# The last convolution pieces handed on inside SBUF, and the last gate moved to the activation, in an S4D and token-mixer kernel

## The chip, the cores and the metric

The kernel runs on one core of a Trainium2 chip. The metric is the device time of one execution in microseconds; smaller is better. The kernel before was run three times: 697.69 us median, 696.94 to 703.69. Inputs and outputs are float32 in HBM.

The engines named below: TensorE (PE in the profile) multiplies matrices, VectorE (DVE), ScalarE (ACT) and GpSimd (POOL) work on elements, SyncE (SP) only issues DMA transfers, which 16 DMA engines carry out. Each engine takes its instructions in the order in which they stand; engines wait for each other through semaphores.

## The reference, cut to what matters

L is 2048 tokens, D is 448 channels, N is 256 states, F is 1792.

```python
x = A_u
mod = (_silu(c) @ w_mod).reshape(c.shape[0], 6, 1, -1)
sa, ca, ga, sb, cb, gb = (mod[:, k] for k in range(6))

# first half: a state-space layer, computed as a long convolution over the tokens
h = _layernorm(x) * (1 + ca) + sa
K = 2.0 * jnp.einsum("dn,dnl->dl", C, jnp.exp((A * dt[:, None])[:, :, None] * pos)).real
y = jnp.fft.irfft(jnp.fft.rfft(h_t, 2 * L) * jnp.fft.rfft(K, 2 * L), 2 * L)[:, :, :L]
x = x + ga * (y + h * D_skip)

# second half: an MLP over the token axis, shared by the channels
h = _layernorm(_layernorm(x) * (1 + cb) + sb)
u = _gelu(jnp.einsum("bsd,sf->bdf", h, w1) + b1)
x = x + gb * (jnp.einsum("bdf,fs->bds", u, w2) + b2)
```

The layer norm is taken twice before the MLP, once outside and once in the mixer. `gb` (in the kernel `mod[5]`) scales channels; the MLP mixes tokens and leaves the channels apart.

## The kernel before, in words

**Up to about 350 us** the kernel makes the convolution kernel K from the state-space parameters (`st_step`, `st_kgen`), transforms it and the normalised input with matrices of sines and cosines, and leaves the transformed input in the HBM tensor `us_d`. The channels are taken in two halves of 224 (`DC`), c = 0 and c = 1.

**The pieces.** Per half there are 16 pieces (`NP`), n = 0 to 31 in all; piece n holds two of the 32 rows k of the outer transform. For a piece, `pc_load` (L768) brings its input `u` and its tables `si`, three pieces ahead, in rings of three and four buffers. `pc_s2` multiplies (`kx`, L804), VectorE makes two products (`z`, L812), `pc_inv` transforms back (`vv`, L820 and L821), and `pc_out` (L823) has ScalarE copy the values from PSUM to the tile `vt` and stores them to the HBM tensor `v_d` (L828). In the second half ScalarE also makes a swapped copy of u (`pc_swap`), and GpSimd builds two of the tables (`pc_tables`, L795 to L797). The pieces of the first half run inside the work on K. Those of the second run in the loop `for k in range(NP + 1)` from L1171.

**The order of SP's queue.** All of these transfers are issued by SP. Up to k = NP - 4 a planner places them; from there on (`tc.manual_schedule(engines={ENG.SP})`) they stand as written. The order of the other engines is written out by hand throughout. At k = NP - 3 SP issues the first weight block of the MLP (`wst.load`, L186) and the first pair of x blocks (`x_pair`, L1166), after the loop the second weight block.

**The token blocks.** The second half of the kernel goes over 16 token blocks, r = 0 to 15, of 128 tokens. `ln_load` (L1228) reads block r's values from `v_d` into a tile `vt` (128 partitions: the 32 rows k times 4; two groups g of 448). `ln_y` (L1246) finishes the inverse transform with the table `ft`, two matmuls, one per group, into one PSUM tile `y`, of which there is a single buffer; VectorE adds it to x and sums the row (L1253). `stats` (L1237) makes the mean on VectorE and then, on ScalarE, the sum of squares of (value - mean) and its root. `ln_mod` applies the gate and takes the second sum and `stats`; `ln_out` writes the normalised block as a rounded part `h3h` and a remainder `h3l`, so that three fast matmuls replace a full-precision one. In front of the first blocks stand matmuls on `acc[6]` that nobody reads (`warm`, L1291: nine, one and two of them before y(0), y(1) and y(2)).

**The MLP.** `WeightStream` loads weight blocks of 128 x 896 (ring of three), and splits each into `whi` (ScalarE, L206) and `wlo` (VectorE, L215). The first sweep runs over the 16 token blocks for the first 896 of the hidden units (`mlp1`, seven PSUM banks, 21 matmuls a block) with the normalisation in between; then `gelu` (L1332) empties the banks into `uh[0]` and `ul[0]` through a ring `u` of three buffers; a second sweep does the other 896 units and `gelu` fills `uh[1]` and `ul[1]`. The third sweep makes 16 output blocks of 128 tokens, each from kh = 0 and kh = 1 (21 matmuls each), and ends each with

```python
V.scalar_tensor_tensor(y, o, b2[:, t : t + 1], mod[5], ALU.add, ALU.mult)
V.tensor_tensor(y, y, xt, ALU.add)
nc.sync.dma_start(out[0, ss], y)
```

where `xt` is the block's x after the first half, parked in HBM (`x2_d`) during the second sweep.

## Time and profile before

| what | value |
|---|---|
| runs of the kernel | 697.69 us median (696.94 to 703.69, three runs) |
| the profiled execution, its own time | 699.5 us |
| its span | 697.7 us |
| TensorE busy | 646.5 us (93%) |
| ScalarE busy | 448.5 us (64%) |
| VectorE busy | 424.1 us (61%) |
| GpSimd busy | 274.7 us (39%) |
| mean granted TensorE clock | 0.988 of full speed |
| HBM traffic | 91.46 MB read, 34.87 MB written, 181 GB/s over the span |

The span runs from the first instruction to the last event of one profiled execution; the time of that execution is somewhat longer than its span. Lines such as L1250 are lines of the kernel before. In the rows of a timeline the columns are: start in us, duration in us, engine, line, operation, output <- inputs, shapes, how many instructions were merged, and in brackets how long the engine had been idle and what ended the wait. "SPq" is SP issuing a transfer; the transfer itself ends later. Adjacent matmuls overlap in the records, so starts tell the pace better than durations. A name such as `w` stands for all buffers of that tile.

### The profile page before, as it was taken

Reading aid. Unit: us, or ns where it says so; the run is one execution under the profiler, and the core shown is the slowest. Engines: PE = TensorE matmul, PEld = TensorE weight load, DVE = VectorE, ACT = ScalarE, POOL = GpSimd, SP = SyncE. Lnnn points to the kernel's source line nnn. Section 1 sums busy time; section 2 is a strip of 40 time slices with the busy share of each in tenths; the row PEclk is TensorE's granted clock in tenths of the full one; section 3 lists DMA queues with packets and bytes.
Section 4 is the critical chain, followed back from the end, with each engine's and each line's share of the span. In section 5 each row is a group of like instructions: output and inputs, shape, how many; then the busy total and the mean of one; then the engine's idle time right before and its main releaser. Section 6 shows DMA issues by size and latency. Waiting matters only on the chain.

```text
span 697.7 us, 18532 instructions
## 1 busy us (share of the span) xinstructions
PE 646.5 (93%) x7314; PEld 486.1 (70%) x7314; DVE 424.1 (61%) x811; ACT 448.5 (64%) x841; POOL 274.7 (39%) x364
## 2 busy tenths in 40 slices
PE   0868999999988899999999989999999999999997
PEld 0444454455545676676789747778999999999996
DVE  7877889787575584857744368777622354444431
ACT  5787698899879899999766568877422332222220
POOL 6694669588588767777546200000000000000000
PEclk9998999999999999999999999999999999999999
DMA  7595647588785486554579899974683445555640
GB/s 183 178 194 143 214 163 241 212 234 268 213 266 165 126 170 170 145 157 120 142 235 301 257 278 244 236 177 135 174 247 108 146 132 159 159 158 165 169 129 28
DMA packets 101894, 128.04 MB, mean 184 GB/s; under 512 B 13547, under 2 KB 85231, under 8 KB 101807
## 3 DMA queue, kind: packets, MB, share of 16 engines
q1 hardware_dynamic: 100606, 123.31, 63.0%
q0 software_dynamic: 1200, 3.54, 2.4%
q8 instruction: 58, 0.95, 0.6%
q14 instruction: 30, 0.24, 0.1%
HBM read 91.46 MB, written 34.87 MB: 181 GB/s over the span
## 4 chain that ended last, share of the span: by engine, by line
PE 68%; ACT 10%; DMA 8%; DVE 6%; issue 4%; POOL 3%; SPq 1%; DVEq 0%; ACTq 0%; POOLq 0%
PE xe L621 7%; PE acc L1222 7%; PE o L1365 6%; PE o L1364 6%; PE o L1366 6%; PE acc L1223 6%; PE acc L1224 6%; PE kg L711 6%; DMA si<-in_SK_dram 3%; PE xg L621 3%; PE pu L542 2%; PE pu L574 2%; PE vv L820 2%; PE kx L804 2%; PE vv L821 2%
## 5 line engine op out<-in xcount | busy, mean ns | idle before, releaser
L206 ACT CAST whi<-w 128x896 fp32r<-128x896 f32 x64 | 59.8, 938 | 134.9 <-PE o L1365 84.6
L215 DVE TENSOR_TENSOR wlo<-w,whi 128x896 fp32r<-128x896 f32 x64 | 68.1, 1088 | 43.1 <-ACT whi L206 36.8
L684 POOL TENSOR_TENSOR G<-mag,gs 128x512 f32<-128x512 f32 x56 | 71.9, 1283 | 50.9 <-ACT gs L680 47.1
L1222 PE MATMUL acc<-h3h,whi 128*128 128x448 f32 x224 | 82.7, 369 | 0.8 <-ACT h3h L1273 0.8
L1223 PE MATMUL acc<-h3l,whi 128*128 128x448 f32 x224 | 81.5, 364 | 0.7 <-DVE h3l L1280 0.5
L1365 PE MATMUL o<-ul,whi 128*128 128x448 f32 x224 | 81.3, 363 | 0.0
L1364 PE MATMUL o<-uh,whi 128*128 128x448 f32 x224 | 81.2, 362 | 0.0
L1224 PE MATMUL acc<-h3h,wlo 128*128 128x448 f32 x224 | 80.7, 360 | 0.0
L1366 PE MATMUL o<-uh,wlo 128*128 128x448 f32 x224 | 80.6, 360 | 0.0
L711 PEld LDWEIGHTS kg<-E,G 128*32 128x32 f32 x3584 | 56.6, 114 | 32.3 <-issue 22.2
L711 PE MATMUL kg<-E,G 128*32 128x64 f32 x3584 | 66.4, 228 | 6.7 <-issue 6.1
L685 POOL TENSOR_TENSOR G<-mag,gs 128x512 f32<-128x512 f32 x56 | 71.8, 1282 | 0.0
L621 PE MATMUL xg<-tab,lph 64*128 64x512 f32 x112 | 62.3, 556 | 5.1 <-ACT gs L680 2.4
L621 PE MATMUL xe<-tab,lph 64*128 64x512 f32 x112 | 62.2, 555 | 1.1 <-ACT gs L681 0.9
L686 DVE TENSOR_TENSOR E<-m,xe 128x512 f32<-128x512 f32 x53 | 36.4, 687 | 41.3 <-ACT xe L679 24.3
L1368 DVE SCALAR_TENSOR_TENSOR y<-o,b,mod 128x448 f32<-128x448 f32 x16 | 10.9, 684 | 80.2 <-PE o L1366 80.2
L665 POOL TENSOR_TENSOR m<-mag,w 128x512 f32<-128x512 f32 x53 | 56.0, 1056 | 4.3 <-DMA u<-us_d 0.2
L1222 PEld LDWEIGHTS acc<-h3h,whi 128*128 128x128 f32 x224 | 42.0, 188 | 13.9 <-ACT h L1278 5.6
L812 DVE TENSOR_TENSOR z<-kx,u 128x448 f32<-128x448 f32 x48 | 28.4, 620 | 27.7 <-PE kx L804 27.7
L1223 PEld LDWEIGHTS acc<-h3l,whi 128*128 128x128 f32 x224 | 42.1, 188 | 3.3 <-DVE h3l L1280 0.8
L1364 PEld LDWEIGHTS o<-uh,whi 128*128 128x128 f32 x224 | 42.0, 188 | 3.4
L621 PE MATMUL xe<-tab,lex 64*128 64x512 f32 x56 | 28.9, 531 | 16.6 <-DMA lex<-wm 15.8
(233 smaller groups left out, 1512.1 us busy)
## 6 DMA issues: line engine op xcount, KB each, us to landing
w<-in_B_w_dram SPq DMA_DIRECT2D x64, 224.0 KB
w<-in_B_w_dram SPq DMA_DIRECT2D x32, 448.0 KB
u<-us_d SPq DMA_DIRECT2D x48, 224.0 KB
yu_d<-yt SPq DMA_DIRECT2D x16, 448.0 KB
yi<-yu_d SPq DMA_DIRECT2D x32, 224.0 KB
us_d<-uo SPq DMA_DIRECT2D x16, 448.0 KB
v_d<-vt SPq DMA_DIRECT2D x32, 224.0 KB
vt<-v_d SPq DMA_DIRECT2D x16, 448.0 KB
```

What stands on the lines that cost most here:

```text
L206: self.nc.scalar.copy(hi, w)
L215: eng.tensor_tensor(lo, w, hi.bitcast(F32), ALU.subtract)
L621: T.matmul(out[k], lhs[r], rhs[r], start=start, stop=stop)
L684: G.tensor_tensor(Gt[:, 1], mg_, v32(sg), ALU.mult)
L685: G.tensor_tensor(Gt[:, 0], mg_, v32(cg_), ALU.mult)
L711: T.matmul(kg[32 * q : 32 * q + 32, m], Gt[:, c, d], E[:, c, d], start=h == 0 and c == 0 and m == 0, stop=h == 1 and c == 1, skip_group_ch ...
L1222: nc.tensor.matmul(acc[f], hi[:, fs], h3h[:, r], start=r == 0, stop=False)
L1223: nc.tensor.matmul(acc[f], hi[:, fs], h3l[:, r], start=False, stop=False)
L1224: nc.tensor.matmul(acc[f], lo[:, fs], h3h[:, r], start=False, stop=r == 15)
L1364: nc.tensor.matmul(o, hi[:, ks], uh[kh][:, k], start=kh == 0 and k == 0, stop=False)
L1365: nc.tensor.matmul(o, hi[:, ks], ul[kh][:, k], start=False, stop=False)
L1366: nc.tensor.matmul(o, lo[:, ks], uh[kh][:, k], start=False, stop=kh == 1 and k == 6)
```

## The change: the first two blocks, the squares and the last gate

1. **The first two token blocks.** The tables of the inverse transform are reordered so that within a piece's 128 rows the block number r is outermost. So block r's rows of a piece lie together, `v_d` is read in runs of two groups (3584 bytes a partition), and the rows of blocks 0 and 1 are the first 16 partitions of each `vt` of `pc_out`. For the last four pieces (n = 28 to 31; k = 24 to 31 of the second half of the channels) SP copies these 16 partitions to an SBUF tile `vlast` before it stores the piece to `v_d`. Blocks 0 and 1 read from `v_d` what was stored earlier: the last rows of the first half in four short transfers, and all of k below 24 in one (`v_load(r, end)`). `ln_y` makes their `y` from four matmuls of 224 columns with `ft` and two with a new table `fl` (128 KB) on `vlast`.
2. **Places in SP's order.** The first two weight blocks and the first pair of x blocks are written ahead of the loop, in the part that the planner places; the second pair of x blocks stands before blocks 2 and 3. In the order that results, the two weight blocks and the first pair are issued behind the u load that stood at 353.10 us, ahead of the tables of piece 19; the four short transfers ahead of the u load of piece 21.
3. **`warm`.** One, two and two matmuls instead of nine, one and two.
4. **`stats`.** ScalarE squares (total - D * value) straight from the row sum, with the scale taken out at the root; the mean is made on VectorE behind that.
5. **The last gate.** `gelu` multiplies the activation by `mod[5]` on VectorE before it is split; in the second half ScalarE makes the rounded part, one slice behind. The third sweep's end multiplies the bias and adds x (in place) without waiting for the matmuls, and then adds the product.

```diff
-    order = lambda a: a.reshape(P, 32, 2, 2, 2, 16).swapaxes(3, 4)
+    order = lambda a: a.reshape(P, 32, 2, 2, 2, 16).transpose(0, 1, 5, 2, 4, 3)
...
+    fl = np.zeros((4, 2, 4, 2, 2, 2, 2, 64))
+    for r in range(2):
+        for g in range(2):
+            fl[:, r, :, g, r, :, g] = t["FT"][-32:].reshape(4, 2, 4, 64).swapaxes(1, 2)
+    t["FL"] = fl.reshape(64, 2 * 2 * P)
...
             rows = v_d[2 * p : 2 * p + 2, :, c * DC : (c + 1) * DC]
+            late = n - 2 * NP + 4
+            if late >= 0:
+                nc.sync.dma_start(vlast[16 * late : 16 * late + 16], vt[0:16])
             nc.sync.dma_start(rows.rearrange("k p d -> p k d"), vt)
...
+        v_v = v_d.rearrange("k (r ch g) d -> r k ch g d", ch=4, g=2)
+        end = 2 * NP - 8
+        wst.load()
+        wst.load()
+        x_pair(0)
+        vlast = swp.tile([64, 2, DC], F32, name="vlast", bufs=1)
+        fl = swp.tile([64, 2, 2, P], F32, name="fl", bufs=1)
+        vts = {}
+
+        def v_tile(r):
+            vts[r] = rot.tile([P, 2, D], F32, tag="vt", name="vt", bufs=4)
+
+        def v_load(r, k):
+            nc.sync.dma_start(vts[r][0 : 4 * k].rearrange("p g d -> p (g d)"), v_v[r, 0:k].rearrange("k ch g d -> k ch (g d)"))
+
         pc_swap(NP)
         for k in range(NP + 1):
...
-            if k == NP - 3:
-                wst.load()
-                x_pair(0)
-
-        wst.load()
+            if k == 1:
+                nc.sync.dma_start(fl.rearrange("p r j m -> p (r j m)"), i["FL"])
+                for r in range(2):
+                    v_tile(r)
+                    for g in range(2):
+                        nc.sync.dma_start(vts[r][4 * end :, g, 0:DC], v_v[r, end:, :, g, 0:DC])
+            if k == NP - 2:
+                v_load(0, end)
+
+        v_load(1, end)
         last.close()
...
         def ln_load(r):
-            vts[r] = rot.tile([P, 2, D], F32, tag="vt", name="vt", bufs=4)
-            nc.sync.dma_start(vts[r], v_v[r])
+            v_tile(r)
+            v_load(r, 2 * NP)
...
             mean, ss, rs = (small(nm, tag) for nm in ("mean", "ss", "rs"))
+            sq = rot.tile([P, D], F32, tag="sq", name="sq")
+            S.activation(sq, src, AF.Square, bias=total, scale=-float(D), accum_out=ss)
+            S.activation(rs, ss, AF.Sqrt, scale=1.0 / D**3, bias=eps_t)
             V.tensor_scalar(mean, total, -1.0 / D, None, ALU.mult)
-            sq = rot.tile([P, D], F32, tag="sq", name="sq")
-            S.activation(sq, src, AF.Square, bias=mean, accum_out=ss)
-            S.activation(rs, ss, AF.Sqrt, scale=1.0 / D, bias=eps_t)
...
+            n = 4 * end
             for g in range(2):
-                nc.tensor.matmul(y[64 * g : 64 * g + 64], ft, vt[:, g], start=True, stop=True)
+                out = y[64 * g : 64 * g + 64]
+                if r > 1:
+                    nc.tensor.matmul(out, ft, vt[:, g], start=True, stop=True)
+                    continue
+                nc.tensor.matmul(out[:, 0:DC], ft, vt[:, g, 0:DC], start=True, stop=True)
+                nc.tensor.matmul(out[:, DC:], ft[0:n], vt[0:n, g, DC:], start=True, stop=False, skip_group_check=True)
+            for j in range(2) if r < 2 else ():
+                nc.tensor.matmul(y[:, DC:], fl[:, r, j], vlast[:, j], start=False, stop=j == 1, skip_group_check=True)
...
-        for r in range(4):
+        x_pair(2)
+        for r in range(2, 4):
             ln_load(r)
-            if r == 1:
-                x_pair(2)
...
-                warm((9, 1, 2)[t + 3])
+                warm((1, 2, 2)[t + 3])
...
         def gelu(acc, fh):
+            us = {}
+
+            def split(f, copy):
+                copy(uh[fh][:, f], us[f])
+                V.tensor_tensor(ul[fh][:, f], us[f], uh[fh][:, f].bitcast(F32), ALU.subtract)
+
             for f in range(7):
                 k = 7 * fh + f
-                u = ru.tile([P, D], F32, tag="u", name="u")
-                S.activation(u, acc[f], AF.Gelu_apprx_tanh, bias=b1[:, k : k + 1])
-                V.tensor_copy(uh[fh][:, f], u)
-                V.tensor_tensor(ul[fh][:, f], u, uh[fh][:, f].bitcast(F32), ALU.subtract)
+                us[f] = ru.tile([P, D], F32, tag="u", name="u")
+                S.activation(us[f], acc[f], AF.Gelu_apprx_tanh, bias=b1[:, k : k + 1])
+                V.tensor_tensor(us[f], us[f], mod[5], ALU.mult)
+                if fh == 0:
+                    split(f, V.tensor_copy)
+                elif f:
+                    split(f - 1, S.copy)
+            if fh:
+                split(6, S.copy)
...
-            V.scalar_tensor_tensor(y, o, b2[:, t : t + 1], mod[5], ALU.add, ALU.mult)
-            V.tensor_tensor(y, y, xt, ALU.add)
+            V.scalar_tensor_tensor(xt, mod[5], b2[:, t : t + 1], xt, ALU.mult, ALU.add)
+            V.tensor_tensor(y, o, xt, ALU.add)
             nc.sync.dma_start(out[0, ss], y)
```

3 lines of the change are left out of this document (1 added, 2 removed).

## The prediction, made before the changed kernel was run

> **What bounds the kernel now.** I read the page first, then the table of TensorE's waits from the last convolution pieces to the end, then the timeline of all engines around the one place where those waits sit.
>
> ```profile
> span 697.7 us, 18532 instructions
> PE 646.5 (93%) x7314; PEld 486.1 (70%) x7314; DVE 424.1 (61%) x811; ACT 448.5 (64%) x841; POOL 274.7 (39%) x364
> ```
>
> TensorE is busy for 93% of the span. Its waits from 392 us to the end are these few (columns: total, times, longest):
>
> ```profile
> PE acc L1222 <- ACT h3h L1273: 0.8, 1, 0.8
> ...
> PE acc L1223 <- DVE h3l L1280: 0.5, 1, 0.5
> ```
>
> From 418 us on the same view has no row for matmuls at all: the three MLP sweeps run without a gap, so work on the other engines is free there as long as it stays ahead, and only three places can move the end: the change-over from the convolution to the MLP, a new stall in the sweeps, and what follows the last matmul. The change-over:
>
> ```profile
> 393.61 0.53 ACT L826 COPY vt<-vv 128x448 f32<-128x448 f32 x1 [1.03 <-PE vv L821]
> 394.16 1.28 ACT L1197 ACT_TABLE_LOAD   x1
> 394.17 0.36 SPq L828 DMA_DIRECT2D v_d<-vt  x1
> 394.20 7.03 PE L1294 MATMUL acc<-mod 128*128 128x448 f32 x18 [0.67 <-ACT vt L826]
> ...
> 395.57 0.92 ACT L206 CAST whi<-w 128x896 fp32r<-128x896 f32 x1
> ...
> 396.52 1.09 DVE L215 TENSOR_TENSOR wlo<-w,whi 128x896 fp32r<-128x896 f32 x1 [0.74 <-ACT whi L206]
> ...
> 397.47 1.22 SPq L1230 DMA_DIRECT2D vt<-v_d  x2
> ...
> 401.37 0.97 PE L1250 MATMUL y<-vt,ft 128*64 128x448 f32 x4
> ...
> 402.39 0.62 DVE L1253 SCALAR_TENSOR_TENSOR xt<-xt,y 128x448 f32<-128x448 f32 x1 [0.92 <-DMA vt<-v_d]
> ...
> 403.06 0.15 DVE L1240 TENSOR_SCALAR mean<-sum 128x1 f32<-128x1 f32 x1
> ...
> 403.29 0.67 ACT L1242 ACTIVATE sq<-xt,mean 128x448 f32<-128x448 f32 x1 [3.00 <-DMA xt<-in_A_u_dram]
> ...
> 406.00 0.61 DVE L1253 SCALAR_TENSOR_TENSOR xt<-xt,y 128x448 f32<-128x448 f32 x1
> ...
> 408.49 0.47 PE L1222 MATMUL acc<-h3h,whi 128*128 128x448 f32 x1 [0.85 <-ACT h3h L1273]
> ```
>
> The last values leave PSUM at 394.14. They go to HBM, come back as the first vt tile, and TensorE fills the time with nine products that nobody reads (L1294). The first residual sum starts at 402.39, the first useful matmul of the MLP at 408.49: 14.35 us after the last copy.
>
> **1. The round trip goes (gain 4.1 us).** In the chain of waits the last store takes
>
> ```profile
> 394.17 3.22 DMA v_d<-vt
> ```
>
> and the reload the rest up to 401.37. After the change a copy of 16 rows (28 KB) is issued at 394.17 in the store's place. I bound its landing above by the store's own 3.22 us, 397.4, though it is an eighth of the bytes; below by nothing. Two 224-column products with `fl` follow; a pair of that size takes 0.92 us (L804, row below), so y is complete by 398.4 at the latest. The four 224-column products with `ft` need only pieces stored earlier; their reload leaves SP behind the store of piece 29, about 391, and with the 3.9 us of the old one (397.47 to 401.37) lands about 395: they run before.
>
> Now ask what is late next. In the program order VectorE has both wlo differences ahead of the first residual sum, and ScalarE has the table load and both whi casts behind the last copy. The weights are there early now, so wlo runs from 396.52 for 2 x 1.09 us: the sum starts at 398.7, whether the copy landed at 396 or at 397.4. The gain is 402.39 - 398.7 = 3.7 us. Taking the square from the sum (`stats`) drops the wait for the mean, twice in this chain: from 403.06 to 403.29 is 0.2 us each time, 0.4 in all. The mean itself stays on VectorE, beside ScalarE's square.
>
> On TensorE, up to the first MLP matmul, stand after y(0): two warm products (7.03 / 9 = 0.78 us each), y(1) with six short products (at most 3 x 0.92), two warm, y(2) (0.97). With y(0) done by about 398.4 that is 398.4 + 1.6 + 2.8 + 1.6 + 1.0 = 405.4 as an upper bound, 404.1 if the 64-column products overlap as L1250's do; ScalarE's h3h comes at 408.49 - 4.1 = 404.4. I take 404.4; the other end costs 1.0 us. The fewer warm products remove only filler. Tile vt 2 must wait for all stores; the last one now follows the copy, about 0.8 us later, so it ends by 398.2, and 3.9 us bring vt 2 at 402.1, before y(2) at about 403.3.
>
> **2. The second block (gain 0.5 us).** The wait on L1280 (0.5 us, above) belongs to block 1, whose square now starts without the mean that VectorE makes only after h3l. I count it gone; if it stays, the cost is that 0.5 us.
>
> **3. The moved loads (loss 2.5 us).** In the order of the changed kernel SP issues w0, w1 and the first x pair, six DMAs, right after the u load of 353.10, ahead of si(19); the four short reloads of the first half's last rows stand ahead of u(21); half of x pair 1 stands ahead of si(30). Before, w0 and x 0 left at 388 and w1 at 394.6, behind all loads of the loop.
>
> ```profile
> 346.40:353.40 7.00, 6.04 (x88) 5.07 (x88) 2.31 (x4) 1.49 (x4) 1.86 (x4) 1.00 0.65 186
> 353.40:361.00 7.60, 7.23 (x37) 6.58 (x37) 3.56 (x6) 6.26 (x12) 3.27 (x6) 1.00 0.72 211
> 361.00:388.00 27.00, 26.51 (x140) 25.92 (x139) 12.91 (x23) 18.77 (x34) 17.80 (x33) 1.00 0.96 298
> ...
> 355.00 0.33 SPq L780 DMA_DIRECT2D si<-in_SK_dram  x1
> 357.91 0.39 POOL L795 COPY si<-si 64x256 f32<-64x256 f32 x1 [1.93 <-DMA si<-in_SK_dram]
> 360.97 0.92 PE L804 MATMUL kx<-yk,si 128*128 128x224 f32 x4
> 365.30 0.39 POOL L795 COPY si<-si 64x256 f32<-64x256 f32 x1 [1.42 <-DMA si<-in_SK_dram]
> 365.51 0.92 PE L804 MATMUL kx<-yk,si 128*128 128x224 f32 x4
> ...
> w<-in_B_w_dram SPq DMA_DIRECT2D x12, 224.0 KB
> ...
> xt<-in_A_u_dram SPq DMA_DIRECT2D x10, 224.0 KB
> ```
>
> (The last numbers of the first three rows: granted clock, DMA share, GB/s.) The DMA engines are 0.96 busy at 298 GB/s from 361 to 388, and si arrives just in time: si(19) 3.1 us before its product, si(21) 0.2 us (365.30 against 365.51). The loop is bound by TensorE and all but bound by DMA as well. The moved bytes are 6 x 224 KB and four times 28 KB, 1.49 MB: 5.0 us at 298 GB/s. Free in 353 to 361 is (0.96 - 0.72) x 7.6 = 1.8 us. So 3.2 us of transfers are pushed into the full stretch, less the 0.2 us of lead. Seen from the queue: si(19) leaves some 3.7 us later (six issues and a wait) and lands about 363 behind the burst, 2 us after its product was due. I take 2.5. Above, with no free time and the half x pair counted (0.8 us), it is 5.8; below, 0, if the engines make it up later in the loop. `fl` itself (128 KB, 0.4 us of DMA) is issued about 346, where the engines are 0.65 busy: free. A sentence on a rule: the Trainium skill, page "DMA: Bandwidth & Descriptors", section "Specifications", gives a fabric ceiling of 435 GB/s; by it the burst would cost an estimated 3.4 us less 1.8 free, and the whole sum would come out about 1 us lower. No row here sustains that rate over such a stretch (298 above), so the row decides.
>
> The rows are also laid out so that a reload is one run of 3584 bytes a partition rather than two of 1792; it saves DMA time from 400 on, where no matmul waits, so I count nothing.
>
> **4. The gate at the activation (loss 1.1 us).** Per slice VectorE gets a 128x448 product more.
>
> ```profile
> 488.08 2.49 ACT L1336 ACTIVATE u<-acc,b 128x448 f32<-128x448 f32 x4 [2.27 <-PE acc L1224]
> 488.75 0.39 DVE L1337 CAST uh<-u 128x448 fp32r<-128x448 f32 x1 [2.42 <-ACT u L1336]
> 489.18 0.63 DVE L1338 TENSOR_TENSOR ul<-u,uh 128x448 fp32r<-128x448 f32 x1
> 489.72 0.39 DVE L1337 CAST uh<-u 128x448 fp32r<-128x448 f32 x1
> ...
> 490.88 0.64 ACT L1336 ACTIVATE u<-acc,b 128x448 f32<-128x448 f32 x1 [0.32 <-DVE ul L1338]
> ```
>
> In the first half a slice costs VectorE 0.97 us (488.75 to 489.72); the product, priced like L1338 with the wait for its result, makes it 1.63. The u ring holds three, so activation f waits for difference f - 3. The first difference ends at 488.75 + 0.66 + 0.43 + 0.62 = 490.46, the fourth (f = 3) at 495.35, and the seventh activation runs from 495.5 to 496.1. TensorE wants that PSUM bank for f = 6 of the next sweep: the first bank was ready at 488.0 after three matmuls of a sweep that pace at 0.2 us, so the next sweep begins at 491.5 and f = 6 at 491.5 + 18 x 0.2 = 495.1. It stalls 1.1 us; 0.6 if the product overlaps the op before it. wlo(18) then ends at 501.2, wanted at 501.3: no more is lost, barely. In the second half ScalarE makes the cast:
>
> ```profile
> 558.68 0.36 PE L1364 MATMUL o<-uh,whi 128*128 128x448 f32 x1
> ...
> 562.16 0.62 DVE L1338 TENSOR_TENSOR ul<-u,uh 128x448 fp32r<-128x448 f32 x1
> ```
>
> the last difference moves from 562.8 to about 564.1; TensorE needs it after 21 + 18 matmuls from 558.68, at 566.5. The cover is kh = 0, 4.2 us of other work; free.
>
> **5. The end (gain 0.7 us).**
>
> ```profile
> 693.28 0.68 DVE L1368 SCALAR_TENSOR_TENSOR y<-o,b,mod 128x448 f32<-128x448 f32 x1 [7.05 <-PE o L1366]
> 694.00 0.63 DVE L1369 TENSOR_TENSOR y<-y,x 128x448 f32<-128x448 f32 x1
> ```
>
> The gated bias now joins x before the matmuls end; behind the last matmul stands one sum: 694.00 - 693.28 = 0.72.
>
> **Sum.** -4.1 - 0.5 + 2.5 + 1.1 - 0.7 = -1.7 us. The profiled execution took 699.5 us around its span of 697.7; the median of the three runs is 697.69. The same difference from the median gives **696.0**.
>
> **Rivals.** (a) The moved loads are hidden (step 3 costs 0 to 0.5): 697.7 - 4.6 + 0.3 + 1.1 - 0.7 = 693.8. For: the engines are 0.72 busy where the burst lands, and 0.96 is not 1. Against: si(21)'s lead of 0.2 us. (b) **Slower:** the burst pays in full, 5.8 us, because u(19) to u(21) and si(19) to si(21) stand behind it on SP, and each later load of the rings of three and four starts only when a delayed product frees its buffer: 697.7 - 4.6 + 5.8 + 1.1 - 0.7 = 699.3. It decides from a delay of 4.2 us on. For: the full stretch; against: the free 1.8 us. (c) TensorE's clock falls, since nine warm products become one:
>
> ```profile
> 50.00:52.00 2.00, 0.00 (x0) 0.00 (x0) 0.48 (x1) 0.99 (x3) 2.00 (x3) 1.00 1.05 206
> 54.00:56.00 2.00, 1.96 (x8) 0.95 (x7) 1.99 (x4) 0.02 (x1) 0.54 (x1) 0.50 0.37 83
> ```
>
> After the idle stretch around 50 us the granted clock was 0.50 from 54 to 59, which would cost some 2.8 us of MLP matmuls: 698.8. Against: between 394 and 404 the changed order still has nine or so microseconds of products, with gaps of about 1 us. The Trainium skill, page "TensorE: Matmul & The Clock Gate", Part 1, says the same of idle windows of about 3.4 us; the rows agree on the half clock, and by that rule these gaps are too short. (d) The copies don't set the start at all, since VectorE's two wlo differences do: that is in the forecast, and it means that a slower copy changes nothing up to 397.7.
>
> **Chances.** Forecast (694.5 to 697.5) 0.55; (a) 0.17; (b) 0.17; (c) 0.07; others, either way, 0.04. The range takes in (a) and (b): 692.8 to 699.8. One per cent is 7 us, about what a measurement of this kernel can tell from no change; no case comes near it, so faster 0.04, within 0.92, slower 0.04.
>
> **What would show it.** The six loads before si(19) and the kx products waiting for si somewhere between 361 and 367; the last vt copy near 396.6 rather than 394.1; the first residual sum right behind the second wlo, not behind the copy; the first MLP matmul 10.3 us behind the end of the last vt copy, where it was 14.35; one stall near 495 behind an activation; a single sum behind the last matmul. I am wrong if the loop ends on time (a), if it slips over 4 us (b), or if the granted clock drops after 400 (c).

## The result, and the profile after

The changed kernel took 702.12 us (median of 20 runs, 698.47 to 705.01) where the kernel before, run beside it, took 698.82 (20 runs, 695.51 to 703.69): a ratio of 1.0043, 95% interval 1.0027 to 1.006. Forecast were 696.0 us and a small gain; it is a small loss of about 3 us, above the upper end of the range, 699.8. The profiled execution took 700.88 us. The page of the changed kernel begins:

```profile
span 699.1 us, 18542 instructions
PE 646.2 (92%) x7316; PEld 486.0 (70%) x7316; DVE 428.5 (61%) x818; ACT 451.8 (65%) x848; POOL 274.6 (39%) x364
```

TensorE does the same 646 us of work and waits longer. The table of its waits, changed kernel, from 340 us to the end (total, times, longest):

```profile
PE kx L809 <- DMA si<-in_SK_dram: 5.4, 3, 4.0
PE y L1282 <- DMA vt<-v_d: 1.1, 1, 1.1
...
PE acc L1249 <- ACT u L1376: 0.7, 1, 0.7
```

The first row is the one to look at. Before, the same view has 0.7 us for si; the longest single waits behind the loop there, 0.8 us each, stood at the change-over and are gone here, with one of 1.1 us for vt in their place. What was taken away at the change-over came back in the loop. The timeline of the changed kernel at both places, and at the gelu and the end (start, duration, engine, operation, idle before it and its releaser):

```profile
349.34 0.32 SPq L777 DMA_DIRECT2D u<-us_d  x1
349.71 2.43 SPq L191 DMA_DIRECT2D w<-in_B_w_dram  x2
352.82 1.17 SPq L191 DMA_DIRECT2D w<-in_B_w_dram  x2
354.10 1.18 SPq L1174 DMA_DIRECT2D xt<-in_A_u_dram  x2
...
356.00 0.38 SPq L785 DMA_DIRECT2D si<-in_SK_dram  x1
...
358.31 3.36 SPq L1218 DMA_DIRECT2D vt<-v_d  x4
361.40 1.02 PE L809 MATMUL kx<-yk,si 128*128 128x224 f32 x4 [3.98 <-DMA si<-in_SK_dram]
...
396.57 0.53 ACT L831 COPY vt<-vv 128x448 f32<-128x448 f32 x1 [1.03 <-PE vv L826]
397.44 0.51 SPq L835 DMA_DIRECT2D vlast<-vt  x1
399.29 0.60 PE L1282 MATMUL y<-vt,ft 128*64 128x224 f32 x4 [1.12 <-DMA vt<-v_d]
399.48 2.09 DVE L220 TENSOR_TENSOR wlo<-w,whi 128x896 fp32r<-128x896 f32 x2 [0.74 <-ACT whi L211]
400.39 1.86 PE L1285 MATMUL y<-vlast,fl 64*128 64x224 f32 x4
402.18 3.35 PE L1328 MATMUL acc<-mod 128*128 128x448 f32 x4
402.28 0.62 DVE L1288 SCALAR_TENSOR_TENSOR xt<-xt,y 128x448 f32<-128x448 f32 x1 [0.71 <-PE y L1285]
...
408.07 0.62 DVE L1288 SCALAR_TENSOR_TENSOR xt<-xt,y 128x448 f32<-128x448 f32 x1 [2.28 <-PE y L1285]
409.05 0.76 ACT L1308 ACTIVATE h3h<-h,mean,rs 128x448 fp32r<-128x448 f32 x1 [2.33 <-DVE mean L1305]
410.57 0.47 PE L1249 MATMUL acc<-h3h,whi 128*128 128x448 f32 x1
...
695.39 0.62 DVE L1414 TENSOR_TENSOR y<-o,x 128x448 f32<-128x448 f32 x1 [7.18 <-PE o L1411]
```

In the loop, si(19) leaves SP 6.7 us after u(18) (349.34 to 356.00; before 1.9, from 353.10 to 355.00), and the kx product that needs it stands 3.98 us. At the change-over the first MLP matmul starts 14.0 us after the start of the last vt copy (14.9 before). The clock falls twice, in the loop behind the wait for si and at the change-over. Windows of the changed kernel (span, busy time of PE, PEld, DVE, ACT and POOL, then granted clock, DMA share, GB/s):

```profile
362.00:364.00 2.00, 2.00 (x9) 1.82 (x8) 1.16 (x2) 1.58 (x3) 1.81 (x4) 0.61 0.84 242
364.00:366.00 2.00, 2.00 (x7) 1.79 (x6) 0.00 (x0) 0.65 (x2) 1.03 (x3) 0.54 0.94 323
...
396.00:398.00 2.00, 1.33 (x5) 0.44 (x3) 0.00 (x0) 1.41 (x2) 0.00 (x0) 1.00 0.69 183
398.00:400.00 2.00, 0.88 (x9) 0.51 (x8) 0.58 (x2) 1.99 (x4) 0.00 (x0) 0.99 0.78 254
400.00:402.00 2.00, 2.00 (x8) 1.17 (x4) 1.57 (x2) 0.28 (x1) 0.00 (x0) 0.50 0.61 168
...
404.00:406.00 2.00, 2.00 (x7) 0.58 (x7) 1.59 (x5) 0.46 (x2) 0.00 (x0) 0.50 0.95 332
406.00:408.00 2.00, 2.00 (x13) 1.09 (x9) 0.00 (x0) 0.69 (x3) 0.00 (x0) 0.80 1.01 244
```

Two executions of one kernel reach the loop some microseconds apart (the profiled one of the changed kernel copies piece 12 at 340.3 us, that of before at 344.1, where the change hasn't begun). So the stages are compared by their lengths, not by their times. In us, from the timelines of all kernels: **loop**, from the start of the vt copy of piece 12 to that of the last; **change-over**, from there to the first MLP matmul; **sweep 1**, from there to ScalarE's table load ahead of the first gelu; **rest**, from there to the end of the span. The last column is the ratio of the times to the kernel before, from 9 to 20 runs. A stage is one execution, the ratio is many: the ratio decides, the stage says where.

| kernel | loop | change-over | sweep 1 | rest | ratio (95%) |
|---|---|---|---|---|---|
| before | 49.5 | 14.9 | 76.0 | 213.2 | 1 |
| after | 56.2 | 14.0 | 74.9 | 213.6 | 1.0043 (1.0027 to 1.006) |
| b1_early | 55.8 | 14.7 | 76.8 | 213.2 | 1.0051 (1.0023 to 1.008) |
| b2_gate | 48.8 | 15.3 | 76.0 | 213.8 | 1.0003 (0.9975 to 1.003) |
| b3_six_small | 51.0 | 16.5 | 76.0 | 213.4 | 1.0006 (0.998 to 1.0032) |
| b4_w0_early | 49.6 | 14.7 | 76.1 | 213.2 | 0.9982 (0.9952 to 1.0012) |
| e1_late | 50.9 | 17.2 | 78.2 | 213.8 | 1.006 (1.0027 to 1.0094) |
| e2_spread | 54.4 | 12.6 | 75.8 | 213.8 | 1.0073 (1.005 to 1.0096) |
| e3_warm | 53.1 | 12.6 | 75.0 | 213.7 | 1.005 (1.0026 to 1.0075) |
| e4_spread_warm | 54.3 | 12.6 | 76.2 | 213.8 | 1.0065 (1.0037 to 1.0094) |
| r1_behind_si | 49.5 | 18.8 | 76.1 | 214.1 | 1.0055 (1.003 to 1.0081) |
| r2_first_reads | 50.6 | 17.4 | 76.8 | 214.0 | 1.0079 (1.005 to 1.0109) |
| r3_short_apart | 50.1 | 17.8 | 78.4 | 213.7 | 1.0054 (1.0028 to 1.008) |
| r4_no_gate | 49.8 | 17.4 | 76.8 | 213.2 | 1.0034 (1.0003 to 1.0064) |
| r5_no_queue_wait | 49.2 | 14.2 | 76.6 | 214.1 | 1.0024 (0.9999 to 1.0048) |
| r6_no_queue_wait_no_gate | 50.1 | 15.0 | 76.1 | 213.2 | 1.0032 (1.0011 to 1.0053) |
| r7_w0_ahead | 51.3 | 13.2 | 76.7 | 214.0 | 1.0006 (0.9982 to 1.003) |
| r8_w0_early_only | 50.3 | 13.0 | 77.6 | 213.2 | 0.9992 (0.9971 to 1.0012) |

How much a stage varies from one execution to the next shows where kernels have the same program in it: the loop is 49.5 and 48.8 us in before and b2, and 49.2, 50.1 and 51.3 in r5, r6 and r7; the change-over is 14.9, 15.3 and 16.5 in before, b2 and b3. So a difference of 1 or 2 us between two profiles shows little by itself.

### The profile page after: what moved, and what is told of

Same layout as the page of the kernel before. It is cut to its first block, busy times and chain, and to the rows that moved or that the text cites. A ratio compares the mean times of both kernels' runs of the same rounds, so it can differ in the third digit from the quotient of the medians.

```text
span 699.1 us, 18542 instructions
## 1 busy us (share of the span) xinstructions
PE 646.2 (92%) x7316; PEld 486.0 (70%) x7316; DVE 428.5 (61%) x818; ACT 451.8 (65%) x848; POOL 274.6 (39%) x364
## 4 chain that ended last, share of the span: by engine, by line
PE 73%; ACT 9%; DMA 7%; issue 4%; DVE 4%; POOL 2%; SPq 1%; DVEq 0%; ACTq 0%; POOLq 0%
PE xe L626 7%; PE acc L1249 7%; PE o L1410 6%; PE o L1409 6%; PE o L1411 6%; PE acc L1250 6%; PE acc L1251 6%; PE kg L716 6%; PE xg L626 3%; DMA si<-in_SK_dram 3%; PE pu L547 3%; PE vv L825 2%; PE kx L809 2%; PE pu L579 2%; PE vv L826 2%
## 5 line engine op out<-in xcount | busy, mean ns | idle before, releaser
L716 PEld LDWEIGHTS kg<-E,G 128*32 128x32 f32 x3584 | 55.2, 112 | 30.4 <-issue 21.1
L716 PE MATMUL kg<-E,G 128*32 128x64 f32 x3584 | 64.7, 224 | 4.7 <-issue 4.1
L1414 DVE TENSOR_TENSOR y<-o,x 128x448 f32<-128x448 f32 x16 | 10.0, 626 | 78.8 <-PE o L1411 78.8
L1251 PEld LDWEIGHTS acc<-h3h,wlo 128*128 128x128 f32 x224 | 42.0, 187 | 3.1
L1411 PEld LDWEIGHTS o<-uh,wlo 128*128 128x128 f32 x224 | 41.9, 187 | 2.9
```

What stands on the lines that cost most here:

```text
L716: T.matmul(kg[32 * q : 32 * q + 32, m], Gt[:, c, d], E[:, c, d], start=h == 0 and c == 0 and m == 0, stop=h == 1 and c == 1, skip_group_ch ...
L1251: nc.tensor.matmul(acc[f], lo[:, fs], h3h[:, r], start=False, stop=r == 15)
L1411: nc.tensor.matmul(o, lo[:, ks], uh[kh][:, k], start=False, stop=kh == 1 and k == 6)
```

## The experiments

The names begin with b for the kernel before with one part of the change, e for the changed kernel with one part undone, r for an attempt to repair it. The first four were to tell the early loads from the fillers.

**e1_late.** The early loads at their old places; the pair of x blocks after them kept behind them.

```
-        wst.load()
-        wst.load()
-        x_pair(0)
...
+            if k == NP - 3:
+                wst.load()
+                x_pair(0)
...
+        wst.load()
         v_load(1, end)
+        x_pair(2)
```

> The changed kernel with the loads of w0, w1 and x0 put back to their places of before (w0 and x0 behind the 14th piece of the second half, w1 behind the loop); x2 is kept behind them, as it was. Theory A (the six early loads of 224 KB stand ahead of si(19) on SP's queue, cost the loop 4.2 us of waiting and another 2.5 us at half clock): from the issue of u(18) to the end of the last vt copy 40.5 us again, as before, where the changed kernel took 47.2; but the 96 rows of vt0 now stand behind about 900 KB of w0 and x0, some 3 us at the 300 GB/s of this stretch, so the change-over is some 3 us longer than in the changed kernel: 698 to 699.5 us in all, level with the kernel before. Theory B (the four short loads of vt, 3.4 us on SP, and fl are what delays the loop): the stretch stays over 44 us and the time is 702 or more.

Measured: 700.89 us (median), ratio 1.006 (1.0027 to 1.0094). The loop is nearly that of before (50.9), as theory A has it: the early loads were most of its loss. But the time did not come back. The change-over grew to 17.2. The timeline of this kernel:

```profile
391.02 0.85 SPq L1189 DMA_DIRECT2D vt<-v_d  x1
...
397.49 1.02 PE L1284 MATMUL y<-vt,ft 128*64 128x224 f32 x4 [4.58 <-DMA vt<-v_d]
```

The 96 rows of vt0 stand behind w0 and x0 and take 6.5 us to come; TensorE waits 4.58 us, and the clock is 0.50 after it. What the loads don't cost in the loop they cost here.

**e2_spread.** The early loads one at a time, in the middle of the loop. (From there on SP's order is written by hand, as it is in e4 and, from k = 4 on, in r3 to r8; the loops of 49.2 to 51.3 us in r3 to r8 show that this alone costs little.)

```
+            if k in (5, 7):
+                wst.load()
+            if k == 9:
+                x_pair(0)
```

> The changed kernel with w0, w1 and x0 loaded one at a time in the middle of the loop (behind the 6th, the 8th and the 10th piece of the second half), SP's order written by hand there. Theory A (the cost lies in six loads at once ahead of si(19)): the stretch from the issue of u(18) to the last vt copy is 40.5 to 41.5 us, and the 96 rows of vt0 land as early as in the changed kernel: 702.1 less 5.7 to 6.7, so 695.4 to 696.4 us. Theory B (the short loads and fl): 700 to 702. Theory C (the loop pays for 1.4 MB wherever it is put): 698 to 700, with waits on si spread over pieces 21 to 27.

Measured: 703.94 us, 1.0073 (1.005 to 1.0096); theory C, with a loss over its range. The timeline of this kernel shows a wait for si behind each of the loads from 372 us on:

```profile
372.71 1.42 SPq L191 DMA_DIRECT2D w<-in_B_w_dram  x2
373.94 1.02 PE L809 MATMUL kx<-yk,si 128*128 128x224 f32 x4 [0.91 <-DMA si<-in_SK_dram]
...
377.83 1.61 SPq L1174 DMA_DIRECT2D xt<-in_A_u_dram  x2
...
380.06 1.02 PE L809 MATMUL kx<-yk,si 128*128 128x224 f32 x4 [1.31 <-DMA si<-in_SK_dram]
...
385.58 1.02 PE L809 MATMUL kx<-yk,si 128*128 128x224 f32 x4 [0.71 <-DMA si<-in_SK_dram]
```

The loop loses 4.9 us, with the clock at 1.00 all through it, where it lost 6.7 with all the loads at once and the clock down. With the loads out of its way the change-over is 12.6 us, 2.3 less than before: that is the round trip's own gain, as far as it shows at this point.

This change-over is worth a closer look. The orders of TensorE, VectorE and ScalarE in it are those of the changed kernel, one filler included, but here the clock stayed up. Two windows and the timeline of this kernel:

```profile
394.00:396.00 2.00, 1.19 (x3) 0.30 (x2) 0.00 (x0) 1.73 (x2) 0.00 (x0) 1.00 0.59 170
396.00:398.00 2.00, 0.61 (x6) 0.51 (x8) 0.90 (x2) 1.95 (x4) 0.00 (x0) 1.00 0.76 251
```

```profile
396.80 0.84 SPq L1189 DMA_DIRECT2D vt<-v_d  x1
...
399.39 0.62 DVE L1290 SCALAR_TENSOR_TENSOR xt<-xt,y 128x448 f32<-128x448 f32 x1
402.39 0.61 PE L1284 MATMUL y<-vt,ft 128*64 128x224 f32 x4 [1.34 <-DMA vt<-v_d]
404.37 0.62 DVE L1290 SCALAR_TENSOR_TENSOR xt<-xt,y 128x448 f32<-128x448 f32 x1 [1.48 <-PE y L1287]
```

The first sum comes 5.1 us behind the start of the last vt copy (394.25 to 399.39), as the prediction had it. But the 96 rows of vt1, asked for behind the last store, take 5.6 us to come (396.80 to 402.39); TensorE waits 1.34 us for them, VectorE's second sum waits 1.48 us, and the first block's last reciprocal stands behind that sum in VectorE's order.

**e3_warm.** Five fillers in place of one ahead of the first block (`warm((5, 2, 2)[t + 3])`).

> The changed kernel with five filler matmuls ahead of the first block in place of one; nothing else. Theory A (TensorE idle ahead of the first block lets the granted clock fall to 0.50 from 400 to 406, which makes fl, the fillers and the second block late and VectorE wait 2.3 us in front of the reciprocal of the first): clock 1.0 there, the first MLP matmul 10.5 to 11.5 us behind the last vt copy (13.5 in the changed kernel), 699 to 700 us in all. Theory B (the chain through ScalarE and VectorE or the landing of vt0 sets it, whatever the clock): 13 to 13.5 us and 702, or slower by the 1.7 us of the fillers.

Measured: 701.39 us, 1.005 (1.0026 to 1.0075). In the profile the clock stays at 1.00 and the change-over is 12.6 where it was 14.0. That the fillers held the clock is not shown: in e2 it stayed up with one. They have a price as well: the first sum comes 6.5 us behind the start of the last vt copy, where it came 5.7 in the changed kernel. In the times no gain can be told from the changed kernel's 1.0043. VectorE's second sum no longer waits.

The first MLP matmul comes 6.07 us behind the first sum (404.41 to 410.48), and 6.10 before (402.39 to 408.49), as if the squares from the sum gained nothing. The rows of `h3h` say otherwise, the first from the kernel before, the second from this one:

```profile
407.68 0.76 ACT L1273 ACTIVATE h3h<-h,mean,rs 128x448 fp32r<-128x448 f32 x1 [0.48 <-DVE mean L1270]
409.33 0.76 ACT L1308 ACTIVATE h3h<-h,mean,rs 128x448 fp32r<-128x448 f32 x1 [0.47 <-DMA xt<-in_A_u_dram]
```

From the first sum to `h3h` it is 5.29 us before and 4.92 here: the 0.4 us of the forecast are there. They don't reach the matmul, because TensorE, without a gap from 398.48 on, is busy with fillers and the next blocks' products until 410.48, 0.4 us behind the end of `h3h`.

**e4_spread_warm.** Both edits.

> Both edits: the loads spread over the middle of the loop, and five fillers ahead of the first block. If both costs are what they are taken for and add up: 702.1 - 6.2 - 2.5 = 693.4 us (692.5 to 694.5), faster than the kernel before by 4 to 6 us. If only the loads cost: 695.5 to 696.5. If neither: 701 to 703.

Measured: 701.66 us, 1.0065 (1.0037 to 1.0094). The sum of 693.4 falls. In the profile the clock is at 1.00 in the loop and at the change-over, and the loop still loses 4.8 us, in five waits for si; the change-over is 12.6, as in e2 with one filler. After these four, theory A was changed: it isn't the place of the loads ahead of si(19) that costs, but that they are in the loop at all, and behind the loop they meet the reads of vt.

**b1_early.** The kernel before, with `wst.load()` twice and `x_pair(0)` ahead of the loop and nothing else.

> The kernel before, with nothing of the change but the place of w0, w1 and x0: loaded ahead of the loop, in front of si(19). By the runs so far the six loads cost the loop 3.6 us where the clock holds and 6.8 where it falls (from the vt copy at 344.1 to the last one: 49.5 us in the kernel before). Theory A (the early place is the loss, and in the kernel before the late loads delay nothing that the first block needs): 698.3 + 3.6 to 6.8 = 702 to 705 us. Theory B (the late loads stand ahead of the reads of vt in the kernel before, so that moving them away gives the change-over 2 to 3 us back): 699 to 702. If the early place costs nothing by itself: 698 or less.

Measured: 702.67 us, 1.0051 (1.0023 to 1.008). This one edit makes a loss of the size of the whole change. The timeline of this kernel, then its windows:

```profile
359.97 0.38 SPq L780 DMA_DIRECT2D si<-in_SK_dram  x1
...
365.82 1.86 PE L804 MATMUL kx<-yk,si 128*128 128x224 f32 x4 [4.37 <-DMA si<-in_SK_dram]
```

```profile
395.00:400.00 5.00, 5.00 (x28) 4.79 (x26) 2.19 (x4) 2.33 (x5) 2.28 (x4) 1.00 0.33 113
400.00:405.00 5.00, 4.33 (x12) 2.20 (x12) 1.94 (x3) 3.69 (x5) 0.00 (x0) 1.00 0.41 114
```

The second fence is the other half of the answer. In this kernel the DMA engines are a third busy at the end of the loop, and yet the change-over is 14.7 against 14.9. The late loads of the kernel before cost it nothing: they filled the time of the round trip. Theory B (a gain at the change-over) is wrong here.

**b2_gate.** The kernel before with the new gate and the shorter end (the diff's `gelu` and its last lines).

> The kernel before, with nothing of the change but the gate at the activation and the shorter end (the multiply behind each gelu, the copies of the second half on ScalarE, one sum behind the last matmul). From the profile of the changed kernel: + 0.7 us in front of the second set of MLP matmuls, - 0.7 behind the last matmul, and about - 0.2 for the rest: 698 to 698.5 us, no change. If the multiply held the second half of the MLP up too: 700 or more.

Measured: 698.7 us, 1.0003 (0.9975 to 1.003): no change, as expected. The table of waits of this kernel has the stall,

```profile
PE acc L1222 <- ACT u L1342: 0.7, 1, 0.7
```

and its matmuls slip by more than this wait: from the first gelu to the start of the last matmul it is 204.80 us before and 205.95 here, 1.15 more. From there to the end of the span it is 4.8 before and 4.3 here. Over all kernels the rest is 213.2 to 213.4 us with the old gate and 213.6 to 214.1 with the new one.

**r1_behind_si.** All loads behind the last si; five fillers.

```
+            if k == NP - 4:
+                v_load(0, end)
+                wst.load()
+            if k == NP - 3:
+                v_load(1, end)
+                v_top(0)
+            if k == NP - 2:
+                x_pair(0)
+                v_top(1)
+        wst.load()
+        x_pair(2)
```

(`v_top(r)` is the pair of short loads of tile r.)

> The changed kernel, with every load for the change-over put behind the last si: the 96 rows of vt0 and w0 behind the 28th piece's store, vt1 and two of the short loads behind the 29th, x0 and the other two behind the 30th, w1 and x2 behind the loop; and five fillers ahead of the first block. Theory A (what stands ahead of si costs the loop, wherever it is, and the round trip itself is a gain): the loop as before, 49.5 to 50 us from the vt copy at 344 to the last; first MLP matmul 12.6 us behind the start of the last vt copy (14.9 in the kernel before); the end 0.7 shorter: 698.3 - 2.3 - 0.7 + 0 to 0.5 = 695.3 to 696 us, faster than the kernel before. Theory B (so many issues on SP in the last four pieces make the stores of the last pieces or x0 late): change-over 15 us or more, 698 to 700 us.

Measured: 701.71 us, 1.0055 (1.003 to 1.0081). Theory B: the loop is that of before to a tenth, 49.5, and the change-over 18.8, 2.9 us of it TensorE waiting for the last short store (the copy to `vlast`): SP issues with hardly a break from 392.5 to 402.9, and that store is one of the last in the line.

**r2_first_reads, r3_short_apart, r4_no_gate.** Fewer issues in the last four pieces. r2:

```
+            if k == NP - 4:
+                v_load(0, end)
+            if k == NP - 3:
+                x_pair(0)
+            if k == NP - 2:
+                v_load(1, end)
+        wst.load()
+        x_pair(2)
+        wst.load()
```

r3 has, besides, the short loads at `k in (5, 7, 9, 11)`, one each; r4 is r3 with the old gate and end.

> The changed kernel, with three things moved: the 96 rows of vt0 are asked for right behind the store of the 28th piece, the last that they need; x0 behind the 29th and vt1 behind the 30th; w0, x2 and w1 only behind the last store. Three fillers ahead of the first block. The four short loads stay where the change put them. Theory A (SP's queue is what has to be kept short, ahead of si and in the last four pieces both): the loop 1.4 us longer than in the kernel before (50.9 from the vt copy at 344 to the last, the short loads' share as the kernel with the late loads had it), the first block's sum 5 to 6 us behind the start of the last vt copy (8.8 in the kernel before), the first MLP matmul 11 to 12.5 (14.9): 698.0 + 1.4 - 2.4 to - 3.9 + 0.5 (gelu) = 695.6 to 697.5 us. Theory B (w0 so late that the split of w0 is the last thing the first MLP matmul waits for): 14 us or more, 699 or more.

> As the one before it, and the four short loads one at a time, behind the 6th, 8th, 10th and 12th piece of the second half, in place of all four ahead of u(21). Theory A (a piece of 2.2 us has room on SP for one load of 0.85 us but not for four in a row): the loop as in the kernel before, 49.5 to 50.2 us, and 694.8 to 696.5 us in all. Theory B (each load on SP delays si by its own 0.85 us, wherever it stands): the loop 50.5 to 52 us and 696 to 698.

> As the one before it, with the gate and the end of the kernel before. From the first gelu to the end the profiles show 213.2 us with the gate of before and 213.6 to 214.0 with the new one: 0.4 to 0.8 us faster than the one before it, 694.2 to 696 us. If the new gate gains what its shorter end shows (0.7): 0.3 to 0.7 us slower than the one before it.

Measured: 703.2, 702.27 and 702.17 us; 1.0079 (1.005 to 1.0109), 1.0054 (1.0028 to 1.008), 1.0034 (1.0003 to 1.0064). None of the three came as expected. On the loop r3's theory A fits (50.1 and 49.8 with one short load to a piece, 50.6 and 50.9 with four in a row in r2 and e1), but r5 to r8, with the short loads apart as well, lie at 49.2 to 51.3, so one profile each does not show it. The change-over is 17.4 to 17.8, by none of the theories given. The timeline of r3 shows why:

```profile
382.99 0.37 SPq L836 DMA_DIRECT2D v_d<-vt  x1
387.26 0.81 SPq L1189 DMA_DIRECT2D vt<-v_d  x1
388.17 0.61 SPq L835 DMA_DIRECT2D vlast<-vt  x1
...
395.15 0.54 SPq L835 DMA_DIRECT2D vlast<-vt  x1
...
398.98 1.83 PE L1289 MATMUL y<-vlast,fl 64*128 64x224 f32 x4 [4.27 <-DMA vlast<-vt]
```

The reload of vt0 has to wait until the 28th piece's store has landed. Issued right behind it, it holds SP's queue for 3.9 us (383.36 to 387.26), and everything behind it, the short stores too: the last one leaves at 395.15 though its copy ended at 391.22. This is the round trip again, moved into the queue. Its products start 3.8 us after that, with TensorE idle for 4.27 us and the clock down to 0.50 behind it.

**r5_no_queue_wait, r6_no_queue_wait_no_gate.** r3, with vt0 one piece later, behind x0, so that the store has landed by then, and five fillers; r6 has the old gate.

```
             if k == NP - 3:
                 x_pair(0)
+                v_load(0, end)
```

> The changed kernel with the short loads one at a time in the loop, no early w0, w1 and x0, and an order in the last four pieces in which no issue on SP has to wait for a store that has just gone out: behind the 29th piece's store x0 and then the 96 rows of vt0, behind the 30th vt1, behind the last w0, x2 and w1; five fillers. In the kernels that asked for vt0 right behind the 28th store, SP stood 4.3 us for that store (383.0 to 387.3) and the last short store was issued 4.5 us behind its copy. Theory A (the stand on SP's queue made the change-over of those kernels long): last vt copy to first block's sum 6.3 to 6.8 us (10.2 in the kernel with the short loads apart, 8.8 in the kernel before), first MLP matmul 12.4 to 13, the loop 50 us: 698.4 - 2 + 0.4 + 0.5 = 697 to 698 us. Theory B (the transfers themselves are the bound: x0, the stores and vt0 are 1.7 MB behind the last si and take 6 to 8 us at the 215 to 270 GB/s of this stretch, in whichever order): sum 9 to 10 us behind the copy, clock at 0.50 while TensorE waits, 701 to 703.

> As the one before it, with the gate and the end of the kernel before: 0.4 to 0.8 us faster than the one before it if the profiles' 213.2 us against 213.6 to 214.0 from the first gelu to the end hold; 0.7 slower if the shorter end is what counts. Theory A of the one before it: 696.2 to 697.6; theory B: 700.5 to 702.5.

Measured: 699.42 us, 1.0024 (0.9999 to 1.0048), and 699.84, 1.0032 (1.0011 to 1.0053). The stand is gone, and r5's change-over is 14.2: between the theories. The first sum comes 7.0 us behind the copy's start (8.8 before), then the split of the late w0 stands in VectorE's order ahead of the first block's second half. The gate makes no difference that these runs can tell; the 0.4 to 0.8 us that r6 was to gain do not show in the time.

**b3_six_small, b4_w0_early.** Bytes or issues: the kernel before with six loads of 28 KB ahead of the loop, into tiles that are loaded in full later, besides the late ones; and with w0 alone early.

> The kernel before, with six more loads ahead of the loop at the place of the early ones, each an eighth of their size (28 KB, into tiles that are loaded in full later; nothing reads these values); w0, w1 and x0 stay late. Theory A (the early loads cost by their bytes, on DMA engines that are full): 0.17 MB at 320 GB/s is 0.5 us, the loop 49.5 to 50.2 us from the vt copy at 344 to the last (55.8 with the full loads), no change in the time, 698 to 699 us. Theory B (by six issues on SP's queue, 0.6 us each, ahead of si(19)): most of the 3.6 us, a wait for si of 2 to 4 us at the 20th piece, 700.5 to 702.

> The kernel before with w0 alone (0.46 MB, two loads) ahead of the loop, x0 and w1 late. By bytes at 320 GB/s: the loop 1.4 us longer, 51 us, and the change-over not shorter, since what the first block waits for there is vt0: 699 to 700 us. If the first 0.46 MB find room in the stretch ahead of si(19), where the DMA engines are 0.66 to 0.76 busy: 49.5 to 50 us and 698 to 698.5.

Measured: 1.0006 (0.998 to 1.0032) and 0.9982 (0.9952 to 1.0012): no loss that can be told from none for either. So it is neither six issues alone (b3's profile is 1.5 us longer in the loop and 1.6 at the change-over, but the times don't bear that out) nor early loading as such; the first 0.46 MB find room. By these two and b1, what costs is the remainder of the bytes, on DMA engines without a gap; no run moved the remainder alone.

**r7_w0_ahead, r8_w0_early_only.** r7 is r5 with w0 between the last short store and the last long one, and the third block's values ahead of w1. r8 has r7's order of those values, w0 alone ahead of the loop, and the old gate and end.

> The kernel without the stand on SP's queue (r5), with w0 asked for between the last short store and the last long one, and the third block's values ahead of w1. In r5 the split of w0 stood in VectorE's order ahead of the first block's second half (1.1 us) and the third block's matmuls waited 1.2 us for their values. If these are what is left: first MLP matmul 13 to 13.3 us behind the start of the last vt copy (14.2 in r5), 1 to 2 us faster than r5, 697.5 to 698.5, level with the kernel before or just under it. If DMA engines at 1.03 to 1.08 busy from 400 to 420 set the first blocks' pace whatever the order: no gain on r5, 699 to 700.

> The kernel with w0 alone ahead of the loop (no cost in b4), the short loads one at a time, x0 and the 96 rows of vt0 behind the 29th piece's store, x2, the third block's values and w1 behind the last store, five fillers, and the gate and end of before. If the round trip is worth what the shorter change-overs showed (first MLP matmul 12.6 us behind the start of the last vt copy, 14.9 in the kernel before) and the short loads cost the loop 0 to 1.4: 696.5 to 698.5 us where the kernel before has 698.5 to 699.5, ratio 0.996 to 0.999. If the gain is eaten in the first blocks of the MLP, whose DMA engines are full from 400 on: ratio 0.999 to 1.003.

Measured: 700.11 us, 1.0006 (0.9982 to 1.003), where the kernel before took 699.58; and 698.17 us, 0.9992 (0.9971 to 1.0012), where it took 699.84. Both level with the kernel before; none beats it by what can be measured. In r8 the change-over is 13.0, 1.9 us shorter than before. What became of them is one row in its table of TensorE's waits from 403 to 486 us; behind it two of its windows:

```profile
PE y L1285 <- DMA vt<-v_d: 2.6, 1, 2.6
```

```profile
405.00:410.00 5.00, 4.29 (x20) 2.75 (x19) 4.50 (x14) 3.69 (x10) 0.00 (x0) 1.00 1.05 250
410.00:415.00 5.00, 3.10 (x15) 2.29 (x16) 3.88 (x11) 3.91 (x9) 0.00 (x0) 1.00 1.05 231
```

The MLP starts earlier and then waits for the values of a later block, on DMA engines that are full: sweep 1 takes 77.6 us against 76.0. The loop is 0.8 longer. In this profile the gain is given back.

## Why the prediction was wrong, by its own steps

The forecast of -1.7 us failed at **step 3**, the moved loads, and at **step 1**, the round trip. Stage by stage the profiles give, for after less before: loop +6.7, change-over -0.9, sweep 1 -1.1, rest +0.4, before rounding +5.2 together; the times say +3.3. Two things by which the prediction was to be known as wrong came: the loop slipped by over 4 us, and the clock dropped after 400. One sign came near by luck: the last vt copy ends at 397.1, and 396.6 was foretold, but only because this execution reached piece 12 some 3.8 us earlier than the one before and then lost 6.7 us in the loop.

**Step 3: the place right, the term too small.** The loads stand where the prediction put them, si is late at the place named, and the free room fits: 1.8 us at 298 GB/s is 0.54 MB, and w0's 0.46 MB cost nothing that can be told (b4). But si(19) left SP 4.8 us later than before, where the step had 3.7, and TensorE stood 3.5 (e3), 4.0 (after) and 4.4 us (b1) for it, where the step had 2. So 2.5 us was taken for the loop where 3.6 was measured with the clock up (e3), 4.9 spread out with the clock up (e2), and 6.3 and 6.7 where the clock fell behind the wait (b1, after). The prediction had weighed the half clock only for the change-over, not for the wait that its own step makes in the loop. The slower rival (b), with 5.8, is near the loop's loss, but not by its mechanism: it gave the free room nothing, and b4 shows room; what takes the loop beyond 5 us in these profiles is the clock. Its 699.3 also kept the whole gain of step 1.

**Step 1: right up to the first sum, wrong from there, and wrong in what it is worth.** Forecast were 5.1 us from the start of the last copy to the first sum, and 5.7 from the sum to the first MLP matmul, a gain of 4.1. Measured were 5.7 and 8.3, a gain of 0.9. The first is close, and in e2, with the clock up, it is 5.1. It holds in the changed kernel although vt0's rows took 4.8 us from their issue (394.50 to 399.29) where the step had 3.9. In the second, two terms are missing from the sum. One is the clock, rival (c): at 0.50 from 400 to 406, it made two fillers 3.35 us long and the second block's products late, and VectorE's second sum, which stands ahead of the first block's last reciprocal in its order, waited 2.28 us. (c) had 0.07, with the argument that gaps of about 1 us are too short; in this execution they weren't. The other is the arrival of vt1: the step asked when the rows of vt0 and vt2 land, and not when those of vt1 do. In e2, with the clock up, they are what TensorE waits for, and it is 7.5 us from the sum to the first MLP matmul. In e3 the fillers take the place of that wait. Both end at 12.6: 2.3 us of the 4.1.

These 2.3 us last where the loads are in the loop (sweep 1 is 75.0 to 76.2 in e2 to e4, and 76.0 before), and there the loop loses more than that. This is the deeper error of the step: it asked what is late next only up to the first MLP matmul, and the round trip was not idle time of the DMA engines. Before, w0, x0 and w1 go through while the values travel, and they delay nothing that shows (b1: with them gone, share 0.33 to 0.41, and no gain). They have to go through somewhere: in the loop they cost si, behind it they stand ahead of vt0 (e1, 4.58 us of waiting) or of a later block's values (r8, 2.6 us in one profile).

**Step 2**: the row is gone, as forecast, but not by the squares alone: r3 and r4, which have them too, show this row again (L1319 there, 0.9 us). The squares themselves, priced in step 1 at 0.4, gain 0.4 up to `h3h` (5.29 and 4.92 us, e3), and TensorE's own order hides it from the first MLP matmul.

**Step 4** (+1.1) and **step 5** (-0.7) came as predicted, in place and size. There is one stall behind an activation, 0.7 us as a wait; from the first gelu to the start of the last matmul it is 204.80 us before and 205.95 after. From there to the end of the span it is 4.82 and 4.11, with one sum behind the last matmul. Together the rest is 0.4 longer, and b2 shows no change in the time.

**Rival (a)**, the hidden loads, is excluded by b1. **(d)**, that a slower copy to 397.7 would change nothing, was not decided: in the profile after, the sum waited 0.71 us for TensorE at half clock, and in e2 the second wlo and TensorE's products end within 0.1 us of each other, just ahead of the sum.

What stays open: how much of the 3.3 us of the times is waiting and how much is clock. A profile is one execution, and the clock falls in some and not in others. The mean granted clock of the 20 runs after is 0.983 and of the 151 runs of the kernel before that were timed beside the experiments 0.987, so the falls are commoner in the changed kernel. In those 151 runs 0.001 less of mean clock goes with about 0.5 us more time; by this, as an estimate, some 2 of the 3.3 us go with the clock, but a wait can cost time and bring the clock down too, so the two aren't parted by it. The waits alone are enough for a loss of this size: e4's mean clock is 0.987, and it is at 1.0065. Also open is how bytes and issues share the loop's loss.

## What to carry to other kernels

A wait for a round trip is only a gain if nothing else uses it: before a transfer is taken out, list what the queue and the DMA engines carry meanwhile, and ask where those bytes go. Here the loads behind the last demand of the full loop were in a good place: moved into the loop, where the DMA engines had been 0.96 busy, they cost it 3.6 us with the clock up and 6.7 where the wait also brought the clock down, while the first 0.46 MB found room. Ask for the arrival of every tile that the new chain needs, the second block's as well as the first's. On an in-order queue, don't issue a reload right behind the store it depends on: everything behind it waits with it, 3.9 us in r3.

## What the runs showed of the hardware

**The clock fell after short gaps.** In the changed kernel TensorE idled 0.67 and 1.12 us between 396 and 399.3, and was 2.2 of 4 us busy; the granted clock was 0.50 from 400 to 406. In e3 it stood 3.49 us in one piece, with no work at all from 362 to 364, and the clock stayed:

```profile
362.00:364.00 2.00, 0.00 (x0) 0.00 (x0) 0.00 (x0) 0.00 (x0) 0.00 (x0) 1.00 1.03 238
366.00:368.00 2.00, 2.00 (x13) 2.00 (x12) 1.16 (x2) 1.60 (x4) 1.81 (x4) 1.00 0.79 233
```

In e2, at the same place as in the changed kernel, the gaps were longer, 0.67 and 1.53 us, TensorE was 1.8 of 4 us busy, and the clock stayed as well (the windows under e2). So neither the length of a gap nor the busy share of such a stretch decides it alone. The Trainium skill, page "TensorE: Matmul & The Clock Gate", Part 1, gives about 3.4 us for the idle window, and says that the window is free-running, so that the moment of a change varies; e3's row fits a window that the gap didn't fill, but 1.8 us of gaps in all, in two pieces, filled none by that figure, and still the clock fell. Here the measurement decides, and the rule behind it isn't known from these runs.

**A small copy is not quickly there.** The last copy of 16 rows (28 KB, SBUF to SBUF) is used 3.8 us after its issue in r3 (395.15 to 398.98, TensorE waiting for it), behind one store of 224 KB that left 0.7 us ahead. TensorE waits for this copy in all of r1 to r8: it is used 3.4 to 4.7 us behind its issue in r2 to r8, and 2.0 us behind it in r1, where the DMA engines were 0.32 busy from 401 to 402 us, around its issue. The 224 KB store of the prediction took 3.22 us. In r2 to r8 an eighth of the bytes saved no time.
